# Joining the scores, sums and products of attention heads into one TensorE visit

## The chip, the cores and the metric

The kernel runs on one core of a Trainium2 chip. The metric is the device time of one execution in microseconds (us). One execution of each kernel was also profiled.

## The reference

Attention over 8 batches of 12 heads, 448 positions and 64 dimensions, with a softmax that has one extra term in its denominator, then a two-layer MoE block with a rational activation:

```python
scores = scale * (q @ k.T);  m = max(scores);  e = exp(scores - m)
attn = e / (sum(e) + exp(-m) + 1e-9);  x = (attn @ v) reshaped to (3584, 768)
h = x @ w_in;  P = a0 + a1*h + a2*h^2 + a3*h^3;  Q = 1 + |b0||h| + |b1|h^2
out = (P / (Q + 1e-6)) @ w_out
```

The kernel leaves the maximum out: it computes exp(scores) / (1 + sum of exp(scores)), with the reciprocal as an exponential of a negative logarithm.

## The kernel before

Heads are handled in pairs `p` (6 per batch) and in quads `qd` (3 per batch). A clock `n = 6*b + p` orders all work. TensorE and ScalarE follow that order exactly. The other engines (VectorE, POOL, SP) are ordered by the scheduler when the kernel is built, which starts an instruction as soon as, by its own estimate, its data and buffers are ready.

```python
def scores(b, h, i):                       # two score matmuls, then exp, 64*112 of the array
    sps = ps.tile([128, 2, 512], F32, tag="sps", bufs=2)
    for half in range(2):
        nc.tensor.matmul(out=sps[0:T, half, 0:S], lhsT=kT[...], rhs=qT[...], ...)
    e = att.tile([T, 2, S], F16, tag="e", bufs=12)
    nc.scalar.activation(out=e, in_=sps[0:T, :, 0:S], func=AF.Exp, scale=scale)

def sums(b, qd):                           # 16 matmuls with ones, 112*32 of the array
    den = ps.tile([128, 512], F32, tag="gen", bufs=4)
    by_heads(den, b, qd, lambda h, j: ones)
    nc.scalar.activation(out=rden, in_=den[:, 0:S], func=AF.Ln, bias=one_c)
    nc.scalar.activation(out=rden, in_=rden, func=AF.Exp, scale=-1.0)

def attend(b, qd):                         # 32 matmuls with v, 112*32; xt = u * rden on VectorE
    for half in range(2):
        u = ps.tile([128, 512], F32, tag="gen", bufs=4)
        by_heads(u, b, qd, lambda h, j: v4[:, h, j, 32 * half:32 * half + 32])
        nc.vector.tensor_tensor(out=xts[b][:, 2 * qd + half, :], in0=u[:, 0:S], in1=rden, ...)

# ... load(b), on POOL: two buffers each of q4, k4 and v4; q4 has two memsets ahead of its loads
# ... transpose_dma(b), on SP: four transposing DMAs that read k4 and q4
# ... store(b, c0, n, src), on SP: one output tile goes out in two pieces

def gemm2(b, tl, nh):
    osb = moe.tile([128, DM], F32, tag="osb")        # two buffers; once per pair of calls
    op = ps.tile([128, 512], F32, tag="gen", bufs=4)
    # ... 16 matmuls
    nc.vector.tensor_copy(out=osb[...], in_=op[:, 0:HD])
    # ... after the second half: store(...)

for at, h, i in ((0.0, 2*p, 0), (0.0, 2*p, 1), (0.5, 2*p + 1, 0), (0.5, 2*p + 1, 1)):
    work.append((n + at, scores, (b, h, i)))
for qd in range(NQ):
    n = b * NP + 2 * qd
    work.append((n + 2.02, sums, (b, qd)))
    work.append((n + 2.52, attend, (b, qd)))
# ... gemm1, MoE element-wise steps, gemm2
```

The softmax here doesn't subtract the row's maximum and nothing guards it: scores larger than these inputs give would overflow.

Of the kernel before, what the change touches and what calls it, by code (L numbers as in the profile page):

```python
# [16 lines left out]
def kernel(  # L17
# [13 lines left out]
    B, H, S, D = q.shape  # L31
    DM, FF = moe_w_in.shape
    NP = H // 2
    NQ = H // 4
# [137 lines left out]
    def scores(b, h, i):  # L172
        qT, kT = loaded[b][3:5]
        sps = ps.tile([128, 2, 512], F32, tag="sps", bufs=2, name="sps")
        for half in range(2):
            r = slice(64 * half, 64 * half + 64)
            c = (4 * h + 1 - half) * T
            nc.tensor.matmul(  # L178
                out=sps[0:T, half, 0:S], lhsT=kT[r, (2 * h + i) * T:(2 * h + i + 1) * T],
                rhs=qT[r, c:c + S], start=True, stop=True,  # L180
            )
        e = att.tile([T, 2, S], F16, tag="e", name="e", bufs=12)
        nc.scalar.activation(out=e, in_=sps[0:T, :, 0:S], func=AF.Exp, scale=scale)  # L183
        ets[b, h, i] = e

    def by_heads(dst, b, qd, w):
        for j in range(NJ):
            for t in range(4):
                nc.tensor.matmul(  # L189
                    out=dst[32 * t:32 * t + 32, 0:S], lhsT=w(4 * qd + t, j),  # L190
                    rhs=ets[b, 4 * qd + t, j // 2][:, j % 2, :],
                    start=(j == 0), stop=(j == NJ - 1), skip_group_check=True,
                )
# [3 lines left out]
    def sums(b, qd):  # L197
        den = ps.tile([128, 512], F32, tag="gen", bufs=4, name="den")
        by_heads(den, b, qd, lambda h, j: ones)
        rden = att.tile([128, S], F32, tag="rden", name="rden")  # L200
        nc.scalar.activation(out=rden, in_=den[:, 0:S], func=AF.Ln, bias=one_c)  # L201
        nc.scalar.activation(out=rden, in_=rden, func=AF.Exp, scale=-1.0)
        rdens[b, qd] = rden

    def attend(b, qd):
        v4 = loaded[b][2]
        rden = rdens.pop((b, qd))
        if qd == 0:
            xts[b] = xp.tile([128, NDC, S], F16, tag="xt", name="xt")
        for half in range(2):  # L210
            u = ps.tile([128, 512], F32, tag="gen", bufs=4, name="u")
            by_heads(u, b, qd, lambda h, j: v4[:, h, j, 32 * half:32 * half + 32])
            nc.vector.tensor_tensor(  # L213
                out=xts[b][:, 2 * qd + half, :], in0=u[:, 0:S], in1=rden, op=ALU.mult
            )
# [20 lines left out]
    def groups(b, gi):  # L236
        last = b == B - 1 and gi == NG - 1
        return [(0, FG // 2), (FG // 2, FG // 2)] if last else [(0, FG)]
# [112 lines left out]
    work = []  # L351
    for b in range(B):
        if b >= 2:
            work.append((b * NP - NP - 1.5, load, (b,)))
            work.append((b * NP - NP - 1.49, transpose_dma, (b,)))
        for p in range(NP):
            n = b * NP + p
            if b < 2:
                work.append((n - 0.95, transpose_pair, (b, p)))
            for at, h, i in ((0.0, 2 * p, 0), (0.0, 2 * p, 1),  # L360
                             (0.5, 2 * p + 1, 0), (0.5, 2 * p + 1, 1)):
                work.append((n + at, scores, (b, h, i)))
        for qd in range(NQ):
            n = b * NP + 2 * qd
            work.append((n + 2.02, sums, (b, qd)))
            work.append((n + 2.52, attend, (b, qd)))
        t0 = (b + 1) * NP + 1.4
        step1 = NP / NFC if b < B - 1 else 0.3
        for fc in range(NFC):
            work.append((t0 + fc * step1, gemm1, (b, fc)))  # L370
            for f0, n in groups(b, fc // FG):
                if fc % FG == f0 + n - 1:
                    args = (b, fc // FG, f0, n)
                    t = t0 + fc * step1
                    for dt, part in ((0.02, den_0), (0.1, den_1), (0.4, num_0),
                                     (0.75, num_1)):
                        work.append((t + dt * (n / FG), part, args))
                    ready = t + 0.5 * n / FG
                    for step in (log, quotient):
                        while slots[0] < ready:  # L380
                            slots.pop(0)
                        work.append((slots.pop(0), step, args))
        t0 = (b + 2) * NP + 3.0
        work.append((t0 - 0.1, left_over, (b,)))
        tiles = list(range(NW)) + ([NW] if b % 2 else [])
        units = [(b, tl, nh) for tl in tiles for nh in range(2)]
        for i, args in enumerate(units):
            work.append((t0 + i * NP / len(units), gemm2, args))
# [34 lines left out]
```

## Time and profile before

| | before |
|---|---|
| median of 3 executions | 470.21 us (469.68 to 471.07) |
| TensorE / VectorE / ScalarE busy | 93% / 78% / 65% of 468.7 us |
| first output GEMM group starts | 104.07 us |
| two later output GEMM groups start at | 193.40 and 214.15 us |

The page of the profile for the kernel before: busy time of each engine, the granted TensorE clock in 40 slices (tenths of full speed), and the chain of waits by engine.

```profile
span 468.7 us, 8030 instructions
PE 436.7 (93%) x3346; PEld 214.3 (46%) x3346; DVE 364.6 (78%) x536; ACT 307.0 (65%) x331; POOL 76.8 (16%) x133
PEclk9999997979999999999999999999999999999989
PE 69%; DMA 10%; DVE 7%; ACT 5%; SPq 5%; issue 1%; POOL 1%; DVEq 0%; POOLq 0%
```

PE is TensorE. The two sevens in the clock row are the two half-speed stretches that the prediction speaks of, between 70 and 106 us.

One quad in the middle, from TensorE's timeline of the kernel before (start, busy us, engine, line, operation):

```profile
234.11 0.59 PE L178 MATMUL sps<-qT,kT 64*112 64x448 f16 x4
234.62 0.94 PE L189 MATMUL den<-e,ones 112*32 112x448 f16 x16
235.49 1.31 PE L224 MATMUL hp<-xt,w_in_sb 128*128 128x448 f16 x6
236.73 0.58 PE L178 MATMUL sps<-qT,kT 64*112 64x448 f16 x4
237.25 1.70 PE L189 MATMUL u<-e,v 112*32 112x448 f16 x32
238.88 1.31 PE L224 MATMUL hp<-xt,w_in_sb 128*128 128x448 f16 x6
```

Read the starts, not the busy times: matmuls overlap. Sums to GEMM takes 0.87 us (235.49 - 234.62). The column `112*32` is the part of the array that is used. It changes at each of these boundaries.

These are the SP queue (the transposing DMAs of batch 5, between two output stores), POOL (loads of k and q for batch 7, v for batch 5) and the start of the same stretch on TensorE, in the kernel before:

```profile
182.17 3.27 SPq L102 DMA_TRANSPOSE qT<-q  x1
185.54 7.42 SPq L105 DMA_TRANSPOSE qT<-q  x1
193.06 1.18 SPq L109 DMA_TRANSPOSE qT<-q  x1
194.28 10.94 SPq L307 DMA_DIRECT2D out_dram<-osb  x5
```

```profile
184.50 2.10 POOL L85 DMA_DIRECT2D k<-in_k_dram  x3 [31.76 <-DMA kT<-k]
196.51 0.43 POOL L68 MEMSET q<- 112x64 f16 x1 [9.92 <-DMA qT<-q]
198.40 2.30 POOL L90 DMA_DIRECT2D v<-in_v_dram  x3
```

### The profile page before, as it was taken

How to read it: one execution, taken by the hardware profiler on the slowest of the kernel's cores; microseconds unless marked ns; L12 is line 12 of the kernel's file. 1: busy time of each engine (PE TensorE's matmuls, PEld its weight loads, DVE VectorE, ACT ScalarE, POOL GpSimd, SP SyncE). 2: the span in 40 equal slices, each digit the busy share in tenths (PEclk: the TensorE clock that was granted, in tenths of full speed). 3: DMA queues.
4: the chain of work that ended last, by engine and by line, in shares of the span. 5: the costliest groups of instructions: out<-in, count | busy, mean ns of one | idle time of the engine just before them, and what ended most of it. 6: DMA issues, size and time to landing. Idle time of an engine off the chain costs nothing.

```text
span 468.7 us, 8030 instructions
## 1 busy us (share of the span) xinstructions
PE 436.7 (93%) x3346; PEld 214.3 (46%) x3346; DVE 364.6 (78%) x536; ACT 307.0 (65%) x331; POOL 76.8 (16%) x133
## 2 busy tenths in 40 slices
PE   2888986979999999999999999999999999999695
PEld 1444432434444454444544444444444445555353
DVE  1234796988999988888989998888989989999800
ACT  2788686667778675659588766658686773566411
POOL 7443003713314001230020001010000000200000
PEclk9999997979999999999999999999999999999989
DMA  9999998999798418991391109811011100110222
GB/s 123 205 205 196 206 169 135 191 180 175 132 167 152 73 31 144 166 149 36 66 184 60 35 0 169 138 34 36 1 34 35 35 23 12 40 48 16 67 69 67
DMA packets 91764, 46.90 MB, mean 100 GB/s; under 512 B 52304, under 2 KB 86608, under 8 KB 91728
## 3 DMA queue, kind: packets, MB, share of 16 engines
q0 software_dynamic: 37136, 22.81, 34.7%
q1 hardware_dynamic: 54592, 23.58, 26.0%
q8 instruction: 26, 0.43, 0.4%
q14 instruction: 10, 0.08, 0.1%
HBM read 45.62 MB, written 11.01 MB: 121 GB/s over the span
## 4 chain that ended last, share of the span: by engine, by line
PE 69%; DMA 10%; DVE 7%; ACT 5%; SPq 5%; issue 1%; POOL 1%; DVEq 0%; POOLq 0%
PE op L322 28%; PE hp L224 24%; PE sps L178 7%; PE u L189 7%; ACT e L183 4%; DMA k<-in_k_dram 4%; PE den L189 4%; SPq L100 3%; DMA q<-in_q_dram 3%; DMA v<-in_v_dram 3%; DMA qT<-q 2%; SPq L102 1%; DVE w L268 1%; DVE g L284 1%; DVE w L273 1%
## 5 line engine op out<-in xcount | busy, mean ns | idle before, releaser
L183 ACT ACTIVATE e<-sps 112x896 f16<-112x896 f32 x192 | 164.6, 915 | 103.8 <-PE sps L178 103.7
L224 PE MATMUL hp<-xt,w_in_sb 128*128 128x448 f16 x768 | 163.4, 357 | 0.6 <-ACT rden L201 0.6
L322 PE MATMUL op<-w_out_sb,g 128*128 128x384 f16 x768 | 133.4, 329 | 3.7 <-DVE g L284 3.7
L224 PEld LDWEIGHTS <-w_in_sb 128*128 128x128 f16 x768 | 68.9, 98 | 84.6 <-issue 31.3
L322 PEld LDWEIGHTS <-g 128*128 128x128 f16 x768 | 75.5, 99 | 57.1 <-DVE g L284 4.4
L232 DVE CAST g<-hp 128x448 f16<-128x448 f32 x112 | 69.1, 619 | 21.0 <-PE hp L224 20.9
L178 PE MATMUL sps<-qT,kT 64*112 64x448 f16 x384 | 64.2, 390 | 15.1 <-ACT e L183 8.7
L279 ACT ACTIVATE c<-c,oneeps_c 128x1792 f16<-128x1792 f16 (+1 forms) x33 | 57.4, 1740 | 14.9 <-DVE c L261 14.9
L283 ACT ACTIVATE c<-c 128x1792 f16<-128x1792 f16 (+1 forms) x33 | 54.5, 1650 | 0.1
L298 POOL COPY gx<-g 128x256 f16<-128x256 f16 x32 | 16.6, 533 | 194.1 <-DVE g L284 131.1
L178 PEld LDWEIGHTS <-kT 64*112 64x112 f16 x384 | 21.1, 129 | 53.0 <-issue 48.5
L284 DVE TENSOR_TENSOR g<-w,c 128x1792 f16<-128x1792 f16 (+1 forms) x33 | 35.5, 1075 | 12.5 <-ACT c L283 12.0
L189 PE MATMUL u<-e,v 112*32 112x448 f16 x768 | 43.0, 368 | 0.0
L261 DVE TENSOR_TENSOR c<-c,w 128x1792 f16<-128x1792 f16 (+1 forms) x33 | 35.1, 1063 | 0.9
L273 DVE TENSOR_TENSOR w<-w,g 128x1792 f16<-128x1792 f16 (+1 forms) x33 | 35.0, 1059 | 0.4
L268 DVE TENSOR_TENSOR w<-w,g 128x1792 f16<-128x1792 f16 (+1 forms) x33 | 34.9, 1056 | 0.4
L213 DVE TENSOR_TENSOR xt<-u,rden 128x448 f16<-128x448 f32 x48 | 29.1, 618 | 6.3 <-PE u L189 6.0
L329 DVE COPY osb<-op 128x384 f32<-128x384 f32 x48 | 26.5, 552 | 5.7 <-PE op L322 5.2
L85 POOL DMA_DIRECT2D k<-in_k_dram x24 | 17.4, 727 | 80.4 <-DMA kT<-k 74.9
L189 PEld LDWEIGHTS <-v 112*32 112x32 f16 x768 | 18.9, 99 | 21.7 <-issue 9.3
L121 DVE COPY qT<-tq 128x896 f16<-128x896 f16 (+1 forms) x12 | 7.6, 632 | 22.9 <-PE tq L119 22.9
L90 POOL DMA_DIRECT2D v<-in_v_dram x24 | 17.5, 732 | 45.0 <-PE u L189 41.8
(37 smaller groups left out, 278.7 us busy)
## 6 DMA issues: line engine op xcount, KB each, us to landing
k<-in_k_dram POOLq DMA_DIRECT2D x24, 224.0 KB, 8.3
q<-in_q_dram POOLq DMA_DIRECT2D x24, 224.0 KB, 7.5
v<-in_v_dram POOLq DMA_DIRECT2D x24, 224.0 KB, 7.4
w_in_sb<-in_moe_w_in_dram POOLq DMA_DIRECT2D x8, 384.0 KB, 12.7
w_out_sb<-in_moe_w_out_dram POOLq DMA_DIRECT2D x1, 3072.0 KB, 26.0
out_dram<-osb SPq DMA_DIRECT2D x8, 336.0 KB, 2.7
out_dram<-osb SPq DMA_DIRECT2D x8, 288.0 KB, 3.1
out_dram<-osb SPq DMA_DIRECT2D x8, 240.0 KB, 2.6
```

Source lines behind the costliest of these rows:

```text
L178: nc.tensor.matmul(out=sps[0:T, half, 0:S], lhsT=kT[r, (2 * h + i) * T:(2 * h + i + 1) * T], rhs=qT[r, c:c + S], start=True, stop=True,)
L183: nc.scalar.activation(out=e, in_=sps[0:T, :, 0:S], func=AF.Exp, scale=scale)
L189: nc.tensor.matmul(out=dst[32 * t:32 * t + 32, 0:S], lhsT=w(4 * qd + t, j), rhs=ets[b, 4 * qd + t, j // 2][:, j % 2, :], start=(j == 0), s ...
L224: nc.tensor.matmul(out=hp[:, 0:S], lhsT=w_in_sb[:, c, fc * 128:(fc + 1) * 128], rhs=xt[:, c, :], start=(c == 0), stop=(c == NDC - 1),)
L232: nc.vector.tensor_copy(out=h, in_=hp[:, 0:S])
L261: nc.vector.tensor_tensor(out=c, in0=c, in1=ns[b, gi, f0], op=ALU.mult)
L268: nc.vector.tensor_tensor(out=m, in0=m, in1=h, op=ALU.mult)
L273: nc.vector.tensor_tensor(out=m, in0=m, in1=h, op=ALU.mult)
L279: nc.scalar.activation(out=c, in_=c, func=AF.Ln, bias=oneeps_c)
L283: nc.scalar.activation(out=c, in_=c, func=AF.Exp, scale=-1.0)
L284: nc.vector.tensor_tensor(out=gs[b, gi][:, f0:f0 + n, :], in0=ns.pop((b, gi, f0)), in1=c, op=ALU.mult)
L322: nc.tensor.matmul(out=op[:, 0:HD], lhsT=lhs(fc), rhs=w_out_sb[:, fc, nh * HD:(nh + 1) * HD], start=(fc == 0), stop=(fc == NFC - 1),)
```

## The change

The intent: take sums and products of a quad right after a score visit, so that the array changes shape once less per quad, and let ScalarE do the sums' logarithm and exponential ahead of the new scores' exponentials, so that VectorE gets `rden` in time. Nothing is added or removed.

```diff
+        return sps
+
+    def exponentials(b, h, i, sps):
         e = att.tile([T, 2, S], F16, tag="e", name="e", bufs=12)
         nc.scalar.activation(out=e, in_=sps[0:T, :, 0:S], func=AF.Exp, scale=scale)
         ets[b, h, i] = e
+
+    def visit(head, before):
+        tiles = [(*head, i, scores(*head, i)) for i in range(2)] if head else []
+        if before:
+            sums(*before)
+        for one in tiles:
+            exponentials(*one)
+        if before:
+            attend(*before)
@@
-            for at, h, i in ((0.0, 2 * p, 0), (0.0, 2 * p, 1),
-                             (0.5, 2 * p + 1, 0), (0.5, 2 * p + 1, 1)):
-                work.append((n + at, scores, (b, h, i)))
-        for qd in range(NQ):
-            n = b * NP + 2 * qd
-            work.append((n + 2.02, sums, (b, qd)))
-            work.append((n + 2.52, attend, (b, qd)))
+            for hh in range(2):
+                first = p % 2 == 0 and hh == 0 and n > 0
+                work.append((n + 0.5 * hh, visit, (
+                    (b, 2 * p + hh), divmod(n // 2 - 1, NQ) if first else None)))
+        if b == B - 1:
+            work.append((B * NP + 0.02, visit, (None, (b, NQ - 1))))
```

## The prediction

> **What bounds it now.** By the page TensorE is busy 436.7 of 468.7 us (93%), VectorE 78%, ScalarE 65%. In windows of 20 us it is busy 19.9 to 20.0 from 100 to 420 us, and the chain of waits runs over its matmuls there. Before that there are two stalls. At 73.8 us it waits 3.75 us for the transposing DMA of batch 2's q (the chain up to 77.6 us is DMA). At 93.5 us it waits 2.47 us for a score tile, because ScalarE stands at a MoE logarithm that waits for VectorE. A half-speed stretch follows each (granted clock 0.84 between 80 and 100 us; 32 products take 3.1 us there, 1.63 elsewhere).
>
> **What the change does.** No instruction is added or removed. Per quad of heads the order on TensorE goes from "scores, sums, GEMM, scores, products, GEMM" to "scores, sums, products, GEMM, scores, GEMM". On ScalarE the sums' logarithm and exponential (0.65 + 0.58 us) now precede the next head's two exponentials (1.72 us).
>
> **Gain 1: array shapes.** The timeline shows 0.87 us for 16 sums matmuls (4 x 0.189 streaming = 0.76), 1.63 for 32 products (1.51), 0.51 for four scores (0.38). The Trainium skill, "TensorEngine Tiling (Array Packing)", Key Properties, says that changing the tiling mode drains TensorE; this trace agrees: about 0.11 us each. Sums and products share 112x32, so a quad goes from 10 changes to 9: 24 x 0.11 = 2.6 us.
>
> **Gain 2: the second stall.** At n = 14, products (1.6 us) move ahead of the wait for the exponentials, filling part of the 2.47 us hole; the exponentials come 1.2 us later, but VectorE gets the previous products earlier. I expect a hole near 1.2 us, possibly without the half-speed stretch behind it: 1 to 4 us gained.
>
> **Losses.** (a) ScalarE now idles during sums and starts exponentials about 2.3 us later in one visit of four. In the closest spacing (sums, products, 6 GEMM matmuls, scores) the next scores need the tile 4.3 to 4.5 us after the visit began; it is free at about 4.45: roughly nothing. (b) Three quads have products followed by 6 GEMM matmuls and scores; with the products gone that spacing falls from 3.4 to 1.75 us and costs 0.27 us each, as 11 such places do now (score groups of 0.85 us): 0.8 us. (c) Batch 2's values are now loaded by POOL before the memset that waits for the q transposes, so near 71 us 0.67 MB competes with the DMA that sets the 77.6 us point: perhaps 2 us lost. (d) VectorE may wait some tenths for rden; four PSUM buffers should hide it.
>
> **Sum.** -2.6 - 2.5 + 0.8 + 2 = about -2.5 to -3: I predict 467.3 us, 8 in 10 between 463.0 and 471.5. Chances: faster by over 2% 0.04, within 2% 0.93, slower 0.03.
>
> **What would show it.** After 110 us, shape changes one fewer per quad, products starting 0.87 us after sums; about 14 score groups of 0.85 us; ScalarE's wait for sums growing to about 20 us in total; the first scores of batch 2 at 77 to 80 us; hole near 95 us shorter, granted clock between 80 and 110 us higher.
>
> **What would make it wrong.** A third half-speed stretch (several us) from a longer early stall; score tiles waiting in many quads because ScalarE is a MoE op behind (1.7 us each); VectorE stalled on rden, late to free PSUM, stopping GEMMs; or the DMA in (c) costing more.

## More of the kernel before

```profile
198.63 0.94 PE L189 MATMUL den<-e,ones 112*32 112x448 f16 x16
199.50 1.31 PE L224 MATMUL hp<-xt,w_in_sb 128*128 128x448 f16 x6
200.65 2.76 PE L322 MATMUL op<-w_out_sb,gx 128*128 128x384 f16 x16
203.34 0.58 PE L178 MATMUL sps<-qT,kT 64*112 64x448 f16 x4
```

POOL's memset of q waits until the q transposes have landed, so its start, 196.5 us, tells when they did. The values' loads come after it. Nothing on TensorE waits here.

## The result, and the profile after

| | before | after |
|---|---|---|
| median of 4 executions | 470.48 us (469.68 to 471.07) | 476.81 us (475.60 to 477.29) |
| ratio | | 1.0132, 95% interval 1.0105 to 1.0158 |
| span of the profiled execution | 468.7 us | 474.6 us |
| first output GEMM group starts | 104.07 us | 104.38 us |
| the output GEMM group at 193.40 us in before (ahead of the stretch) | 193.40 us | 193.68 us |
| the one at 214.15 us in before (behind it) | 214.15 us | 220.69 us |

A ratio here is the mean time of one kernel's runs over that of the other's in the same rounds, so it is not quite the ratio of the quoted medians. Beside the change, the kernel before was measured a fourth time. The change is slower by 1.3%, where I had foretold 467.3 us.

The last three rows settle where: matched by count of matmuls, the two traces are 0.3 us apart until 193 us and 6.5 us apart at 214 us. The page after:

```profile
span 474.6 us, 8034 instructions
PE 439.0 (93%) x3346; PEld 220.0 (46%) x3346; DVE 364.5 (77%) x536; ACT 306.8 (65%) x331; POOL 75.4 (16%) x133
PEclk9988998989999999979999999999999999999999
PE 68%; ACT 11%; DVE 11%; SPq 3%; DMA 3%; issue 2%; POOL 1%; DVEq 0%; POOLq 0%
```

The busy shares hardly moved. The clock row has a new 7 in its 18th slice, at about 200 us. TensorE's timeline of the kernel after in that stretch:

```profile
198.91 0.94 PE L201 MATMUL den<-e,ones 112*32 112x448 f16 x16
199.68 0.93 PE L201 MATMUL u<-e,v 112*32 112x448 f16 x16
203.26 1.69 PE L201 MATMUL u<-e,v 112*32 112x448 f16 x16 [2.65 <-DVE osb L341]
205.51 2.40 PE L236 MATMUL hp<-xt,w_in_sb 128*128 128x448 f16 x6 [0.57 <-DVE g L244]
207.71 3.87 PE L334 MATMUL op<-w_out_sb,gx 128*128 128x384 f16 x16
211.51 0.59 PE L178 MATMUL sps<-qT,kT 64*112 64x448 f16 x4
```

The second half of the products waits 2.65 us for a buffer in PSUM (where the matmuls write their results) that VectorE (DVE) has not emptied, and the next GEMM 0.57 us. Then the matmuls run at half speed: the GEMM of 6 takes 2.20 us from start to start (1.15 before), the output GEMM 3.80 us (2.69), the 16 products 1.68 us (0.82 at full speed, half of 1.63). The sum is 2.65 + 0.57 + 1.05 + 1.11 + 0.86 = 6.24 us, which is the whole loss.

Why did VectorE not empty the buffer? From the totals of waits of the kernel after between 185 and 210 us (waiter, what ended the wait; total us, times, longest):

```profile
DVE osb L341 <- DMA out_dram<-osb: 5.2, 1, 5.2
PE u L201 <- DVE osb L341: 2.7, 1, 2.7
```

One copy into an output tile `osb` waits 5.2 us for the store that still reads that tile. In the kernel before all such waits together were 0.4 us. It had little to spare, though: there the same copy started at 196.77 us, 0.2 us after that store had landed. The chain of waits of the kernel after, in order of time, runs through that store and the transposes ahead of it on SP:

```profile
185.49 8.82 SPq L105
...
194.41 1.18 SPq L109
195.59 0.05 issue
195.64 6.93 DMA out_dram<-osb
...
202.65 0.56 DVE osb L341
```

And POOL of the kernel after in the same stretch:

```profile
184.53 2.36 POOL L85 DMA_DIRECT2D k<-in_k_dram  x3 [30.55 <-DMA kT<-k]
186.89 2.13 POOL L90 DMA_DIRECT2D v<-in_v_dram  x3
202.50 0.15 POOL L68 MEMSET q<- 112x64 f16 x1 [13.48 <-DMA qT<-q]
```

The loads of batch 5's values have moved from 198.4 to 186.9 us, into the middle of the q transposes. These land at 202.5 instead of 196.5 us. The issue of the longest takes 8.82 instead of 7.42 us, and the store behind them starts 1.4 us later. It lands 6.9 us after its start, the same store of the kernel before 2.3 us after its own. That is not a slower store: in each of the 13 traces it lands within about 0.1 us after the q transposes, wherever the loads are and whether that is 2.3 or 7.1 us after its start. It lands when they do.

The loads moved because the products of a batch's last quad come half a slot earlier, which frees that batch's v4 buffer earlier, and the scheduler then found the loads ready before the memset. The Trainium skill, "DMA: Bandwidth & Descriptors", Issuing engines are not separate DMA queues, says that transfers of all issuers run on the same 16 engines and interleave; the landing 6.0 us later, with the loads among the transposes, agrees with that. So the theory is: *early loads on POOL delay transposes on SP, the store behind them, VectorE, TensorE, and then its clock*. The rivals are that the visit order itself (products at once, late exponentials) costs the time, and that the clock dropped by chance.

### The profile page after: what moved, and what is told of

Read it like the earlier page. It is cut to its first block, busy times and chain, and to the rows that moved or that the text cites. A ratio compares the mean times of both kernels' runs of the same rounds, so it can differ in the third digit from the quotient of the medians. Undisturbed runs are those within 1.5% of the kernel's fastest.

```text
span 474.6 us, 8034 instructions
## 1 busy us (share of the span) xinstructions
PE 439.0 (93%) x3346; PEld 220.0 (46%) x3346; DVE 364.5 (77%) x536; ACT 306.8 (65%) x331; POOL 75.4 (16%) x133
## 4 chain that ended last, share of the span: by engine, by line
PE 68%; ACT 11%; DVE 11%; SPq 3%; DMA 3%; issue 2%; POOL 1%; DVEq 0%; POOLq 0%
PE op L334 26%; PE hp L236 23%; ACT e L186 9%; PE sps L178 8%; PE u L201 6%; PE den L201 4%; SPq L105 2%; DMA out_dram<-osb 1%; DMA q<-in_q_dram 1%; DVE c L273 1%; DVE g L244 1%; DVE w L280 1%; DVE g L296 1%; ACT c L291 1%; DVE c L266 1%
## 5 line engine op out<-in xcount | busy, mean ns | idle before, releaser
L178 PE MATMUL sps<-qT,kT 64*112 64x448 f16 x384 | 66.3, 390 | 15.9 <-ACT e L186 12.9
L178 PEld LDWEIGHTS <-kT 64*112 64x112 f16 x384 | 23.5, 128 | 55.4 <-issue 47.9
L310 POOL COPY gx<-g 128x256 f16<-128x256 f16 x32 | 14.6, 478 | 203.9 <-DVE g L296 134.1
L225 DVE TENSOR_TENSOR xt<-u,rden 128x448 f16<-128x448 f32 x48 | 28.3, 618 | 23.1 <-ACT rden L214 12.3
L213 ACT ACTIVATE rden<-den,one_c 128x448 f32<-128x448 f32 x24 | 15.2, 633 | 44.5 <-PE den L201 44.5
L201 PEld LDWEIGHTS <-v 112*32 112x32 f16 x768 | 21.4, 101 | 20.8 <-issue 6.4
L201 PE MATMUL den<-e,ones 112*32 112x448 f16 x384 | 24.8, 382 | 0.0
```

Of the source, the lines that this page charges most:

```text
L178: nc.tensor.matmul(out=sps[0:T, half, 0:S], lhsT=kT[r, (2 * h + i) * T:(2 * h + i + 1) * T], rhs=qT[r, c:c + S], start=True, stop=True,)
L201: nc.tensor.matmul(out=dst[32 * t:32 * t + 32, 0:S], lhsT=w(4 * qd + t, j), rhs=ets[b, 4 * qd + t, j // 2][:, j % 2, :], start=(j == 0), s ...
```

## The experiments

Eleven runs followed, two of them of the two kernels again. All gave correct results. "Held" below means a tiny ScalarE read of v4, half a slot after the last products, which keeps the buffer occupied and so returns the value loads to where they were.

| run | median (range) us | before beside it | ratio, 95% interval |
|---|---|---|---|
| a_hold5 | 469.98 (469.39 to 471.76) | 467.16 | 1.0057, 1.0002 to 1.0112 |
| a_hold | 470.76 (469.75 to 470.93) | 467.16 | 1.0063, 1.0011 to 1.0115 |
| b_one_quad | 472.42 (468.14 to 473.47) | 467.16 | 1.0086, 1.0016 to 1.0155 |
| a_osb3 | 469.53 (467.08 to 470.08) | 467.16 | 1.0024, 0.9957 to 1.0090 |
| before_again | 469.68 (465.91 to 471.20) | 468.99 | 1.0036, 0.9977 to 1.0094 |
| after_again | 476.49 (476.31 to 477.81) | 468.99 | 1.0190, 1.0139 to 1.0241 |
| a_hold_swap | 468.37 (465.04 to 471.32) | 468.99 | 1.0008, 0.9941 to 1.0075 |
| late_merge | 465.73 (463.25 to 466.95) | 468.99 | 0.9947, 0.9892 to 1.0003 |
| late_merge_osb3 | 465.88 (462.61 to 468.18) | 469.69 | 0.9913, 0.9873 to 0.9952 |
| a_osb3_swap | 468.30 (466.78 to 469.91) | 469.69 | 0.9973, 0.9941 to 1.0006 |
| a_split_one | 474.21 (470.81 to 476.37) | 469.38 | 1.0107, 1.0007 to 1.0207 |

The first eight ran on one chip, the next two on a second, the last on a third. Beside the first eight the kernel before took 464.45 to 470.10 us, a wider spread than in the first series; before_again shows where it arises.

### a_hold5: only batch 5's value loads put back

```diff
+    def hold_values(b):
+        nc.scalar.activation(out=junk, in_=loaded[b][2][:, 0, 0, 0:2], func=AF.Copy)
@@
+        if b == 3:
+            work.append(((b + 1) * NP + 0.55, hold_values, (b,)))
```

> The changed kernel with one tiny ScalarE read of batch 3's values half a slot after their last use, so that only batch 5's value loads return behind the q loads on POOL, as before the change. Theory (load order): those loads, started at 187 us in the middle of the q transposes, push the transposes and the output store queued behind them from about 196 to 202 us; VectorE waits 5.2 us for that store, TensorE 3.2 us, and a half-speed stretch follows, 6.3 us in all. Then this run gives 470.5 us (469.5 to 471.5) and no wait of osb for its store. Rival (visit order): the merged visits and late exponentials cost it; then it stays at 476 to 477. Rival (chance of the clock): half-speed stretch comes elsewhere, 473 or more.

The order of TensorE and VectorE is that of the change, and on POOL only these three loads have moved. POOL in a_hold5:

```profile
183.21 2.44 POOL L85 DMA_DIRECT2D k<-in_k_dram  x3 [30.47 <-DMA kT<-k]
196.87 0.15 POOL L68 MEMSET q<- 112x64 f16 x1 [11.22 <-DMA qT<-q]
199.55 2.26 POOL L90 DMA_DIRECT2D v<-in_v_dram  x3
```

The loads are back at 199.6 us, the transposes land at 196.9 us, no osb copy waits for a store, TensorE is busy 24.88 of the 25 us between 190 and 215 us (21.72 in the change), and the time is 469.98 us. On the same chip, in the next series, the change takes 476.49 us (after_again): 6.5 us for three loads in another place. The visit order as the cause of these 6 us falls. Against the kernel before beside it a_hold5 is still 0.6% slower, by an interval just clear of 1; where that lies is not shown.

### a_hold: all value loads put back

```diff
+        if b + 2 < B:
+            work.append(((b + 1) * NP + 0.55, hold_values, (b,)))
```

> The same tiny read for every batch, so that all value loads come after the q loads they overtook. Theory: the early loads of batch 2 hardly matter, because TensorE was itself late at 81 us, so 470 us (467.5 to 471); if the load at 69.5 us did hold back batch 2's q transposes on the critical path, 467 us or less. Rival (visit order): 476 to 477.

470.76 us, no better than a_hold5. So the other early loads, those of batch 2 at 69 us among them, cost nothing that shows in the time. (Batch 3's loads, early in the kernel before too, move back as well, from 106 to 117 us.) This was as the first theory had it, at the upper end.

### b_one_quad: the kernel before with one early product group

```diff
-            work.append((n + 2.52, attend, (b, qd)))
+            work.append((n + (2.03 if b == 3 and qd == NQ - 1 else 2.52), attend, (b, qd)))
```

> The kernel before, with only one of its 24 product groups (batch 3, last quad) moved half a slot earlier, which puts batch 5's value loads ahead of the q loads on POOL and changes no other load. Theory (load order): the whole loss appears, 476 us (474.5 to 477.5), with VectorE waiting about 5 us for the output store near 200 us. Rival (visit order): one visit of 24 cannot matter, 470 to 471.

This is the mirror image: in the kernel before, one of 24 product groups moves, and with it, among the loads, only those of batch 5's values. From the totals of waits of b_one_quad between 185 and 210 us:

```profile
DVE osb L329 <- DMA out_dram<-osb: 5.9, 1, 5.9
PE op L322 <- DVE osb L329: 2.5, 1, 2.5
```

The whole chain of waits appears, with the transposes at 201.95 us. The time rose by 0.9%, not by the 1.3% to 1.9% of the change: a miss of the size. The granted clock stayed 1.00 between 190 and 215 us in this trace, so the loss there is the stall alone, 3.3 us, of which 2.53 and 0.38 us are waits (matched by count of matmuls, the output GEMM group at 193.40 us of the kernel before comes 0.63 us earlier here, the one at 207.77 us 2.63 us later). The half-speed stretch is thus a second, separate step.

### a_osb3: a third output tile, loads left early

```diff
-        e = att.tile([T, 2, S], F16, tag="e", name="e", bufs=12)
+        e = att.tile([T, 2, S], F16, tag="e", name="e", bufs=10)
@@
-            osbs[b, tl] = moe.tile([128, DM], F32, tag="osb", name="osb")
+            osbs[b, tl] = moe.tile([128, DM], F32, tag="osb", name="osb", bufs=3)
```

> The changed kernel with three output tiles instead of two (room taken from the exponentials' tiles, 10 instead of 12, all that the merged visit holds). The loads stay in the changed order. Theory: the transposes and the store are as late as in the changed kernel, but nothing waits for the store, so 470.5 us (469 to 471.5), no osb wait. If the loss comes instead from late transposes holding up scores or from visit order: 475 to 477.

The transposes are as late as in the change (the memset starts at 202.43 us), the store still starts at 195.7 us, but VectorE does not wait for it, TensorE is busy 24.88 of 25 us there, and the time is 469.53 us. So the late transposes alone hurt nobody; the loss passes through the output tile. Without taking room from the exponentials' tiles, a third output tile does not fit: a build of the change with bufs=3 alone is refused, because the tiles do not fit into SBUF.

### before_again and after_again: both kernels once more

> The kernel before, unchanged, for a second trace of it and to see how far two series of it on one chip differ: ratio 1.000 +- 0.005. If the spread of 464 to 470 us seen in the last series is real, the trace will show it before 110 us (the load of batch 2 and the half-speed stretches), not after.

> The changed kernel, unchanged, beside the others on this chip: 475 to 477 us if the store wait near 200 us is there in each execution. With it the loss that load order makes is measured on one chip: about 6 us over a_hold_swap.

before_again was profiled in one of its shorter executions (465.91 us). Its first output GEMM starts at 99.51 us, 4.56 us before that of the first trace, and every later one that I matched, to 422 us, is ahead by 4.55 or 4.56 us. So these two executions differ only ahead of 104 us. Between 70 and 110 us the clock was 1.00, 1.00, 0.83 and 1.00 in stretches of 10 us, against 0.79, 0.87, 0.82 and 0.84 in the first trace. after_again shows the change's loss a second time: an osb wait of 5.3 us and a clock of 0.86 between 190 and 215 us.

### a_hold_swap: exponentials ahead of the sums' logarithm

```diff
         tiles = [(*head, i, scores(*head, i)) for i in range(2)] if head else []
-        if before:
-            sums(*before)
         for one in tiles:
             exponentials(*one)
+        if before:
+            sums(*before)
         if before:
             attend(*before)
```

(on top of a_hold)

> The changed kernel with the values' loads held back for all batches and, on ScalarE, the new scores' exponentials again ahead of the sums' logarithm and exponential. Theory: in the changed kernel eight score groups of 0.67 us (against 0.59) wait for a late exponential; with exponentials first they go back to 0.59, about 0.7 us less than a_hold between 110 and 400 us, and 13 groups of 0.85 stay. It also removes ScalarE's idle time for sums in the first 50 us, where ScalarE is the busiest: sps of batch 1 should be 2 to 4 us earlier. Total 467 to 470 us. If the sums' logarithm needs to be first (products' tiles held up by rden), VectorE waits for rden and TensorE for PSUM: 471 or more.

It tests the second half of the change. I counted TensorE's groups of four score matmuls that start between 110 and 400 us by their busy time (some records can be missing):

| | 0.58 or 0.59 us | 0.67 or 0.68 us | 0.85 us |
|---|---|---|---|
| before | 54 | 0 | 10 |
| after | 43 | 8 | 13 |
| a_hold | 43 | 8 | 13 |
| a_hold_swap | 50 | 0 | 13 |

A group of 0.67 us has waited about 0.09 us for an exponential, one of 0.85 us about 0.26 us. The eight short waits go away with the exponentials first. VectorE waits longer for `rden` in total (28.2 us in 13 waits, 12.3 us in 8 in the change), but between 110 and 190 us TensorE pays nothing for it. Matched by count of matmuls, the lead of a_hold_swap over the kernel before grows by 0.31 us between the output GEMM groups at 104 and 193 us (3.51 to 3.82 us), that of a_hold by 0.04 us (1.35 to 1.39 us). So "sums first" was not needed for TensorE. The trace still lost about 2 us near 195 us to the output store (3.4 us osb wait): this execution was ahead there, and the store was not. So the wait for the store does not need early loads: here VectorE, being early, reached that tile 3.4 us before the transposes and the store had landed.

### late_merge and late_merge_osb3: keep what paid

```diff
-                first = p % 2 == 0 and hh == 0 and n > 0
+                first = p % 2 == 0 and hh == 0 and n > 2 * NP
@@
+            if b < 2:                      # batches 0 and 1 in the order of before
+                work.append((n + 2.02, sums, (b, qd)))
+                work.append((n + 2.52, attend, (b, qd)))
```

(on top of a_hold_swap, held from batch 2 on; late_merge_osb3 also has a_osb3's two lines)

> As a_hold_swap, but the quads of batches 0 and 1 in the order of before (sums and products in separate visits), merged visits from batch 2 on. Theory: the first 77 us are as in the kernel before and the rest gains 0.11 us per quad less 0.26 at three of them: 0.5 to 1.5 us less than before on this chip, 465 to 469. If merged visits help around 95 us (a second stall of the kernel before), the first 110 us will be no better than a_hold_swap.

> late_merge (values' loads held back, old order in batches 0 and 1, merged visits with exponentials first from batch 2) with three output tiles and 10 exponential tiles. late_merge still lost about 2 us near 195 us to the output store; with a third tile that is gone. The 10 exponential tiles may hold up batches 0 and 1, but those end at the loads of batch 2. Theory: 1 to 3 us less than late_merge, 462 to 466 us, 0.985 to 0.995 of before. If the store was not the cause of that loss: as late_merge, 465 to 467.

late_merge took 465.73 us, 0.9947 of the kernel before, whose interval just reaches 1. late_merge_osb3 took 0.9913 of it (0.9873 to 0.9952): it beats the kernel before, though its median is no lower than that of late_merge in the other series, so that the third tile adds anything to late_merge is not shown. It had no wait of VectorE for a store. In late_merge the osb copy started at 194.62 us, after 2.7 us of waiting, just as that store had landed, and TensorE lost 1.3 us.

### a_osb3_swap: the change with two small repairs

```diff
(a_osb3's two lines, and a_hold_swap's swap, on the change; loads early)
```

> The changed kernel with three output tiles (10 exponential tiles), and the exponentials ahead of the sums' logarithm; the values' loads stay early. Theory: no osb wait, no score groups of 0.67 us, so 0.5 to 2 us less than a_osb3 (469.5): 466.5 to 469, the same as before within 0.5%. If sums first is what makes merged visits work: 470 or more.

468.30 us, 0.9973 (0.9941 to 1.0006). The loads are still early. With the store's grip on VectorE gone and the exponentials first, the merged visit is level with the kernel before, perhaps a little better. Its trace gains 1.20 us on the kernel before between the output GEMM groups at 104 and 394 us (0.11 to 1.31 us); 17 quads at 0.11 us less three score groups at 0.26 us would be 1.09 us.

### a_split_one: does the clock drop belong to the products?

```diff
-        if before:
+        if before and before != (4, 0):
             attend(*before)
@@
+        if b == 4:
+            work.append((b * NP + 2.52, attend, (b, 0)))
```

> The changed kernel, with one of its 24 merged visits split again: sums of batch 4's first quad where they are, products half a slot later, so that the stall on the output store near 200 us meets an output GEMM as in b_one_quad and not the products. The loads stay early, so the store is late as before. Theory A (the half-speed stretch of 3 us after the stall belongs to a stall inside the products): VectorE still waits about 5 us for the store, TensorE about 2.5 us, but no half-speed stretch; 473 us (472 to 474.5), granted clock 1.00 in 190 to 215 us. Theory B (it follows from the length or place in time of the stall): clock 0.86 there, 476 to 477.5. If there is no wait for the store at all, load order is not what delays it: 470.

The stall now meets an output GEMM, as in b_one_quad. TensorE's timeline of a_split_one:

```profile
200.35 1.31 PE L236 MATMUL hp<-xt,w_in_sb 128*128 128x448 f16 x6
204.02 4.44 PE L334 MATMUL op<-w_out_sb,gx 128*128 128x384 f16 x16 [2.35 <-DVE osb L341]
208.39 0.59 PE L178 MATMUL sps<-qT,kT 64*112 64x448 f16 x4
```

In this execution (476.18 us) the output GEMM ran at half speed for most of its length, 4.37 us from start to start instead of 2.69. Theory A falls: the stretch does not need a stall inside the products. Theory B, a clock of 0.86 each time, is not borne out as it stands (0.93 in this trace): the four executions took 476.18, 472.24, 476.37 and 470.81 us with mean clocks of 0.974, 0.980, 0.974 and 0.987. A stall of 2.35 us was followed by half speed here, one of 2.53 us in b_one_quad was not. All eight executions of the change took 475.6 us or more, and both of its traces have the stretch.

The kept traces show what goes with it (each trace holds the list of its clock changes, and `prof` with --windows gives busy time and granted clock of each piece). In all 13, every stretch of one granted clock, the last excepted, lasts a whole number of 3.41 us. So the clock changes on a grid of 3.41 us, and the grid lies differently against the program in different executions. Between 60 and 430 us, 26 cells of the grid at full speed had TensorE busy for at most half their length; half speed followed 25 of them (not one of 42% in late_merge), and none of the 1350 busier ones. The change's stall left TensorE busy for 0.90 of the 3.41 us of one cell (199.71 to 203.12 us), that of a_split_one for 1.06 us. The stall of b_one_quad fell into two cells, busy for 2.49 and 1.81 us, and the clock stayed full. Whether a stall of this length costs 3 us more is thus a matter of where it falls on the grid, which is luck. No run moved a stall on purpose to test this.

## Why the prediction was wrong, point by point

- **Bound.** TensorE bounds the kernel after 100 us: right, and unchanged.
- **Gain 1, "24 x 0.11 = 2.6 us".** The unit was right. In the kernel after, one quad, TensorE's timeline:

```profile
241.05 0.94 PE L201 MATMUL den<-e,ones 112*32 112x448 f16 x16
241.82 1.69 PE L201 MATMUL u<-e,v 112*32 112x448 f16 x32
243.44 1.31 PE L236 MATMUL hp<-xt,w_in_sb 128*128 128x448 f16 x6
244.68 0.67 PE L178 MATMUL sps<-qT,kT 64*112 64x448 f16 x4
```

  Sums now take 0.77 us to the next start instead of 0.87, products 1.62 instead of 1.63, so a quad saves 0.11 us. (My sign "products starting 0.87 us after sums" contradicted my own sum; it should have read 0.76.) But of 17 quads between 110 and 400 us, about 1.9 us in all (17 x 0.11), little was kept: about 0.7 us went to eight late exponentials (8 x 0.09) and 0.8 us to three more crowded score groups (3 x 0.26). The trace of a_hold5 gains 0.56 us against the kernel before from 104 to 394 us.
- **Loss (a), "roughly nothing".** Mis-sized: eight waits of 0.09 us. The score group of 0.67 us above is one of them. ScalarE's wait for sums was 44.5 us in total, not 20, but only those eight waits reached TensorE after 110 us.
- **Loss (b), 0.8 us.** Right: 13 groups of 0.85 us instead of 10.
- **Gain 2, the second stall.** The hole shrank from 2.47 to 1.42 us, near my 1.2. The half-speed stretch behind it stayed (clock 0.83 between 100 and 110 us in both traces of the change): the hole fell into one cell of the grid, in which TensorE was busy for 1.58 of 3.41 us, while a hole of 1.38 us in a_hold5 left 1.98 us busy and full speed. And the stage ahead of it became slower: batch 2's first scores start at 81.17 us instead of 77.56. At the first output GEMM the change is 0.31 us behind the trace of before. The gain of 2.5 us did not come. As before_again shows, this stage varies by 4.6 us between executions of one kernel, so two traces could not have settled 2.5 us anyway.
- **Loss (c), the step that failed.** I read in POOL's order that batch 2's values were loaded earlier, put 2 us on it, and counted the cost of early loads only there, where TensorE waits for the transposes. The same reordering moved the loads of batches 4 and 5, and I did not look at those. The runs showed that batch 5's loads delayed the q transposes from 196.5 to 202.5 us, and that an output store, behind them on SP, landed with them. Its tile blocked VectorE for 5.2 us, and with only four PSUM buffers TensorE stood for 3.2 us and then lost 3.0 us at half speed. This term, 6.2 us, was missing from the sum. a_hold5 takes it away, b_one_quad brings its stall into the kernel before, a_osb3 cuts it at the tile. At batch 2 itself the 2 us did not show: the transposes landed at 81.3 instead of 77.8 us, but TensorE, held up by ScalarE, reached those scores only at 81.2 us and did not wait for them.
- **Loss (d), "four PSUM buffers should hide it".** They hid the waits for rden but not a VectorE wait of 5.2 us.
- **"What would make it wrong"** named "a third half-speed stretch", "late to free PSUM" and "the DMA in (c) costing more". At 200 us a half-speed stretch and late PSUM did come, as one chain, but not from the causes named: not from an early stall, not from rden, and not from the loads of (c). Their place on the list is no credit to the reasoning.

## What to carry to other kernels

When a change frees a buffer earlier, look for every load that the scheduler can now start earlier, in every batch, and ask what other transfers will be under way then and what stands behind them in the same queue. A store queued behind slow transfers holds its tile, and the engine that wants the tile stands, as VectorE did here for 5.2 us. A third output tile cost nothing but space and made that chain harmless. Before crediting a saving per instruction, check at each place whether the next wait would take the saving back.

## What the Trainium skill lacked or had wrong

- "TensorEngine Tiling (Array Packing)", Key Properties, says that changing the tiling mode drains TensorE, with no size. Here one change from 112x32 to the next shape cost 0.10 us (sums to the next start 0.87 us with it, 0.77 us without).
- "TensorE: Matmul & The Clock Gate", Part 1 and the table under Why this matters for your kernels, asks for no idle gaps over about 3 us. Here half speed followed gaps of 2.65 us (after) and 2.35 us (a_split_one), and did not follow one of 2.53 us (b_one_quad). The measured gaps are shorter than the rule. The page's free-running window of 3413 ns fits the traces: the clock changed on a grid of 3.41 us, and half speed followed cells in which TensorE was still busy for up to half the time (25 of 26 such cells), so what counts here is how a gap falls on the grid and not its length alone.
- "DMA: Bandwidth & Descriptors", Issuing engines are not separate DMA queues, is borne out, but it has no size for a transposing DMA next to plain loads. Here three value loads (224 KB each) issued during the transposes went with a landing 6.0 us later (202.5 instead of 196.5 us), and a 96 KB store issued behind the transposes on SP landed within about 0.1 us after them in all 13 traces, 2.3 to 7.1 us after its start.
- No page says how far the start of a load-bound kernel varies: the kernel before was 4.6 us earlier in one trace than in another, all of it before 104 us.
